# Identity transposes in TensorE's planned idle time, with a new load model and a new search of the order

## The chip, the cores and the metric

The kernel runs on one core of one Trainium2 chip. The metric is the device time of one execution in microseconds (us): the median of several runs, with one profiled execution beside them.

## What is computed

Everything is float32 at the interface. An attention over 4 batches, 8 heads, 576 positions and 64 dimensions with rotary embedding is followed by two dense blocks over the 2304 tokens:

```python
q_rot, k_rot = rotate(q), rotate(k)
scores = q_rot @ k_rot.T / sqrt(64)
attn = exp(scores - max); attn = attn / (sum(attn) + 1e-9)
x = attn @ v                                    # 2304 tokens x 512
x = ((x @ w1) * (x @ w2)) @ w3 @ w_out          # d_ff 1024
h = maximum(maximum(x @ m1, x @ m2), x @ m3)    # d_ff 768
out = h @ m_out                                 # 2304 x 512
```

## The kernel before, in words

Heads are worked on in 16 pairs (two heads side by side on 128 partitions). Every operand of a matmul is split into a high and a low part in a rounded format, and three products of parts are summed (TERMS), so one logical product is three matmuls.

For each pair there are these steps. `prepare` (line 517) loads the rotated halves of keys and queries (tiles qk; for pair 1 a tile named early), multiplies by the tables of cosines and sines (tabs, line 542), adds (544) and splits (548, 549) into the tile st. `prepare_v` splits the values (559, 561). `score` (567) makes scores into the PSUM tiles s (two of them, two banks each), VectorE takes the row maximum (590), ScalarE the exponential (593). The last 64 rows of both heads are scored together (the common score, operand z). `move` (620) transposes probabilities on TensorE against the identity (`tr`, 597; tile t), ScalarE and VectorE split them into pt (636, 637), and `values` (641) multiplies by v into pv. `collect` and `rows_done` (651, 663) sum and scale the result into xh.

Beside the pairs run the weights. `convert` (418) loads 64-bit words of a weight (raw) and makes split float32 of it on ScalarE, VectorE and POOL. `fold` (463) multiplies w3 and w_out into one matrix, eight times twelve matmuls in tiles m; `gates` (486) multiplies x by w1 and w2, in m too. After the last pair the PSUM pools are exchanged (`open_left`, 734) and the two dense blocks follow (lines 779 to 1046).

Until that exchange PSUM has eight banks: four for the two s tiles, and four shared ones (`banks = Share(4)`, line 384) from which up to two m, two t and one pv take a bank each when they are first written and give it back after their last reader.

No order is written by hand. Every instruction group is a task with an engine, a duration and a priority. `Plan.order` (193) plays all tasks through a model of the engines: on each engine the ready task with the smallest priority comes next, and this gives the static order in which the program is written for each queue (PE, ACT, DVE, POOL and SP, from which all loads and stores are issued by `load`, 375). TensorE's durations are those of full pace (0.109 us for a transpose). `Plan.issue` (281) first shakes the priorities: for each number in MOVES, `move` (84) draws from it a stretch of the order and adds random amounts to some priorities there. The list MOVES holds the numbers that a search kept. Of loads the model says:

```python
if k.tail:                                        # lines 253 to 255
    dma = max(dma, end + 0.65) + 1.2 * k.tail     # tail: 0.82 for 288 KB, 1.46 for a weight's 512 KB
    end = dma + 0.8
```

The identity (ident, line 392, load at line 706) is the second load issued.

Of the kernel before, what the change touches and what calls it, by code (L numbers as in the profile page):

```python
# [10 lines left out]
F32 = mybir.dt.float32  # L11
# [18 lines left out]
TN = 384  # L30
NU = NT // TN
NG = NU // 2

# [8 lines left out]


MOVES = (
# [24 lines left out]
)  # L71


# [9 lines left out]

def move(prio, place, seed):

    d = draws(seed)

    def uni():
        return (next(d) >> 11) * (1.0 / 9007199254740992.0)

    by = (0.1, 0.3, 0.6, 1.5)[next(d) >> 62]
    share = (0.01, 0.03, 0.1, 0.3)[next(d) >> 62]
    parts = (1, 8, 32, 128)[next(d) >> 62]
    width = len(prio) / parts
    lo = uni() * (len(prio) + width) - width
    hi = lo + width
    if parts == 1:
        share *= 0.3
    for i in range(len(prio)):
        if lo <= place[i] < hi and uni() < share:  # L100
            x = uni() + uni() + uni() + uni() - 2.0
            prio[i] = prio[i] + by * 1.7 * x


class Task:
    __slots__ = ("eng", "dur", "emit", "prio", "tail", "deps", "after", "out", "next", "fresh", "shared", "num", "lock")


class Buf:
# [26 lines left out]
class Plan:  # L136
# [6 lines left out]
    LAT = {"PE": 0.05, "ACT": 0.035, "DVE": 0.035, "POOL": 0.08, "SP": 0.1, "HOST": 0.0}  # L143
    LAP = {"PE": 0.0, "ACT": 0.1, "DVE": 0.08, "POOL": 0.04, "SP": 0.0, "HOST": 0.0}
    DRAIN = 0.165

    def __init__(self):
        self.tasks, self.rings = [], []
# [6 lines left out]
    def add(self, eng, dur, emit, r=(), w=(), part=(), deps=(), prio=0.0, tail=0.0, lock=None):  # L155


        k = Task()
        k.eng, k.dur, k.prio, k.tail = eng, dur, prio, tail
        k.lock = eng == "POOL" if lock is None else lock  # L160
        k.num, k.out, k.next = len(self.tasks), [], []
        need = set(deps)
        after, fresh = set(), []
        for b in r:
            need.update(b.writers)
        for b in list(w) + list(part):
            if b.first is None:
                b.first = k
                fresh.append(b)
        for b in w:  # L170
            need.update(b.users)
        for b in part:
            after.add(b.first)
        need.discard(k)
        after.discard(k)
        for b in list(r) + list(w) + list(part):
            b.users.append(k)
        for b in list(w) + list(part):
            b.writers.append(k)
        k.deps, k.after = need, after  # L180
        k.fresh = [b for b in fresh if b.ring.share]
        k.shared = list({id(b): b for b in list(r) + list(w) + list(part) if b.ring.share}.values())

        def go():
            for b in fresh:
                b.t = b.make(b.slot)
            emit()

        k.emit = go
        self.tasks.append(k)  # L190
        return k

    def order(self, prio):

        tasks, LAT, LAP = self.tasks, self.LAT, self.LAP
# [4 lines left out]
        for k in tasks:  # L200
            for b in k.shared:
# [2 lines left out]
                live[b.ring] = 0  # L204
                free.setdefault(b.ring.share, [(0.0, n) for n in range(b.ring.share.slots)])
                wait.setdefault(b.ring.share, [])
        clock = dict.fromkeys(LAT, 0.0)
        soon = {e: [] for e in clock}
        now = {e: [] for e in clock}
        dma, port, done = 0.0, 0.0, []  # L210
        for k in tasks:
            if not left[k.num]:
                heapq.heappush(soon[k.eng], (0.0, k.num))
        while len(done) < len(tasks):
            best = None
# [28 lines left out]
                live[b.ring] += 1  # L244
            if k.lock:
                at = max(at, port)
            end = at + k.dur
            if k.lock:
                port = end
# [1 line left out]
            if e == "PE":  # L251
                end += self.DRAIN
            if k.tail:
                dma = max(dma, end + 0.65) + 1.2 * k.tail
                end = dma + 0.8
            done.append(k)
            for b in k.shared:
# [16 lines left out]
            for o in k.next:  # L274
                ready[o.num] = max(ready[o.num], at)
                left[o.num] -= 1
                if not left[o.num]:
                    heapq.heappush(soon[o.eng], (ready[o.num], o.num))
        return clock["PE"], done, slot

    def issue(self):
        for ring in self.rings:
            if ring.share:
                for a, b in zip(ring.all, ring.all[1:]):
                    if ring.inorder:
                        b.first.after.add(a.first)
                continue
            for n in range(ring.bufs, len(ring.all)):
                b = ring.all[n]
                if b.first is not None:  # L290
                    b.first.deps.update(ring.all[n - ring.bufs].users)
        for k in self.tasks:
            k.after -= k.deps
            for d in sorted(k.deps, key=lambda d: d.num):
                d.out.append(k)
            for d in sorted(k.after, key=lambda d: d.num):
                d.next.append(k)
        prio = [k.prio for k in self.tasks]
        place = {k.num: i for i, k in enumerate(self.order(prio)[1])}
        for seed in MOVES:  # L300
            move(prio, place, seed)
        best = self.order(prio)
        for b, n in best[2].items():
            b.slot = n
        for k in best[1]:
            k.emit()

# [23 lines left out]
def fused_kernel(ctx, tc, qk, vv, cs, w3t, wo, w12, m2, wo2, out):  # L331
# [70 lines left out]
    rb_r = ring(ap, [128, S], F32, "rb")  # L402
    x_r = [ring(ap, [128, n], F32, f"x{i}_") for i, n in enumerate(PN)]
    s_r = ring(ps_a, [128, 2, 512], F32, "s", 2)
    t_r = ring(ps_m, [128, 512], F32, "t", 2, banks)
    pv_r = ring(ps_m, [128, 512], F32, "pv", 1, banks)

# [189 lines left out]
    def tr(o, x):  # L597
        pe.transpose(o, x, ident.t)  # L598

    def inverse(p):  # L600

        sm, prio = sms[p], 2 * p + 2.3
# [100 lines left out]
    for p in range(NP):  # L703
# [5 lines left out]
        for part in range(2):  # L709
# [4 lines left out]
            for j in range(2 + part):  # L714
                score(p, part, j)
            attend(p, part)
    attention = list(plan.tasks)

    for i in range(2):
# [397 lines left out]
```

## Time and profile before

| what | value |
|---|---|
| median of 3 runs | 935.26 us (934.38 to 936.12) |
| the profiled execution: time of its own | 933.76 us |
| its span, first to last instruction | 931.7 us |
| PE busy | 892.7 us, 96% |
| DVE busy | 601.5 us, 65% |
| ACT busy | 495.5 us, 53% |
| POOL busy | 397.6 us, 43% |
| mean granted TensorE clock | 0.992 |

PE is TensorE's matmuls, PEld its weight loads, DVE VectorE, ACT ScalarE, SP the queue of SyncE. Busy shares are averages over the span; the stretches of the section below take it apart. [...] The granted clock is a share of TensorE's full clock. A row's bracket says how long the engine was idle before it and what ended that.

### The profile page before, as it was taken

To read this page: it belongs to the slowest core of one execution; us is meant where nothing else is said; L and a number is where in the kernel's file an instruction comes from. 1 tells how busy PE (TensorE), PEld (TensorE's weight loads), DVE (VectorE), ACT (ScalarE), POOL (GpSimd) and SP (SyncE) were. 2 spreads that over 40 slices of the span, in tenths; PEclk is the share of its full clock that TensorE was granted. 3 is DMA by queue.
4 is the path that set the end of the run, shared out by engine and by line. 5 is a ranking of instruction groups with operands and counts; after the bars stand their busy time and mean duration, and the time that the engine had idled before them with its cause. 6 is when DMAs were issued, how large, how long until landed. Compare 5 with 4: busy or idle time off the path is not lost.

```text
span 931.7 us, 16391 instructions
## 1 busy us (share of the span) xinstructions
PE 892.7 (96%) x6018; PEld 836.9 (90%) x6018; DVE 601.5 (65%) x1048; ACT 495.5 (53%) x1108; POOL 397.6 (43%) x387
## 2 busy tenths in 40 slices
PE   2788989999999999999999999999999999999998
PEld 1577879998999999999998999999999999999886
DVE  6788888886666676567657233656788478578300
ACT  3688888886666667576655132534423333334411
POOL 2778887787745567352110000434653333232000
PEclk9799999999999999999999999999999999999999
DMA  7244556463322223311048343333333214155511
GB/s 276 85 126 164 177 187 200 128 188 101 100 91 75 69 84 99 100 41 32 27 146 273 117 142 92 103 101 96 91 91 130 63 46 147 46 184 175 214 62 68
DMA packets 61088, 110.32 MB, mean 118 GB/s; under 512 B 6736, under 2 KB 39760, under 8 KB 61008
## 3 DMA queue, kind: packets, MB, share of 16 engines
q1 hardware_dynamic: 61008, 109.28, 36.4%
q8 instruction: 47, 0.77, 0.4%
q14 instruction: 33, 0.27, 0.1%
HBM read 83.76 MB, written 25.50 MB: 117 GB/s over the span
## 4 chain that ended last, share of the span: by engine, by line
PE 86%; DVE 6%; ACT 2%; DMA 2%; issue 2%; POOL 1%; SPq 0%; DVEq 0%; ACTq 0%
PE q L373 46%; PE m L373 17%; PE t L598 9%; PE s L373 7%; PE pv L373 7%; DVE sm L590 1%; DVE pt L637 1%; ACT pt L636 1%; DVE cw L439 1%; DMA qk__118<-in_qk_dram 1%; DMA raw<-in_w_dram 1%; DVE raw L437 1%; DMA wq_d<-fl 1%; DVE early L542 0%; DMA wp<-wq_d 0%
## 5 line engine op out<-in xcount | busy, mean ns | idle before, releaser
L637 DVE TENSOR_TENSOR pt<-t,pt 128x320 fp32r<-128x320 f32 (+3 forms) x256 | 131.9, 527 | 58.4 <-ACT pt L636 54.1
L636 ACT CAST pt<-t 128x320 fp32r<-128x320 f32 (+3 forms) x256 | 112.5, 459 | 52.1 <-PE t L598 36.1
L373 PE MATMUL pv<-pt,v 128*128 128x256 f32 (+1 forms) x576 | 115.4, 317 | 4.5 <-DVE pt L637 3.6
L590 DVE TENSOR_REDUCE sm<-s 128x1 f32<-128x576 f32 x144 | 104.2, 749 | 17.3 <-PE s L373 16.4
L373 PE MATMUL q<-gt,wp 128*128 128x384 f32 x576 | 100.0, 334 | 0.0
L373 PEld LDWEIGHTS q<-gt,wp 128*128 128x128 f32 x576 | 99.8, 188 | 0.0
L373 PE MATMUL s<-st 64*128 64x288 f32 x768 | 74.2, 320 | 21.2 <-ACT st L548 13.1
L373 PEld LDWEIGHTS pv<-pt,v 128*128 128x128 f32 x576 | 83.5, 190 | 11.4 <-DVE pt L637 7.5
L373 PEld LDWEIGHTS s<-st 64*128 64x128 f32 x768 | 56.9, 193 | 35.3 <-ACT st L548 13.1
L959 ACT COPY tmp<-q 128x384 f32<-128x384 f32 x54 | 25.9, 480 | 92.6 <-PE q L373 92.1
L373 PE MATMUL q<-yc__7828,u 128*128 128x384 f32 x378 | 72.2, 340 | 0.0
L373 PE MATMUL q<-yc__8073,u 128*128 128x384 f32 x378 | 71.2, 340 | 0.0
L373 PE MATMUL q<-yc__7521,u 128*128 128x384 f32 x378 | 70.5, 340 | 0.0
L972 POOL TENSOR_TENSOR tmp<-tmp 128x384 f32<-128x384 f32 x27 | 30.2, 1119 | 86.9 <-ACT tmp L959 86.9
L373 PEld LDWEIGHTS q<-yc__8073,u 128*128 128x128 f32 x378 | 67.1, 188 | 0.1
L373 PEld LDWEIGHTS q<-yc__7828,u 128*128 128x128 f32 x378 | 67.2, 188 | 0.0
L373 PEld LDWEIGHTS q<-yc__7521,u 128*128 128x128 f32 x378 | 67.1, 188 | 0.0
L373 PE MATMUL q<-tail,tail 128*128 128x512 f32 x216 | 49.1, 389 | 0.0
L373 PEld LDWEIGHTS q<-tail,tail 128*128 128x128 f32 x216 | 40.5, 188 | 8.4
L985 DVE TENSOR_TENSOR tmp<-q,tmp 128x384 f32<-128x384 f32 x54 | 29.8, 554 | 16.3 <-PE q L373 16.2
L900 POOL TENSOR_TENSOR yx<-yc__7521 128x384 f32<-128x384 f32 x2 | 2.7, 1336 | 88.1 <-DVE yc__7521 L884 85.8
L1045 ACT COPY ga<-q 128x512 f32<-128x512 f32 x18 | 10.6, 588 | 54.8 <-PE q L373 46.7
(1282 smaller groups left out, 2149.9 us busy)
## 6 DMA issues: line engine op xcount, KB each, us to landing
gt<-g_d SPq DMA_DIRECT2D x24, 384.0 KB
raw<-in_m_dram SPq DMA_DIRECT2D x72, 128.0 KB
raw<-in_w_dram SPq DMA_DIRECT2D x16, 512.0 KB
h_d<-top SPq DMA_DIRECT2D x36, 192.0 KB
tail<-h_d SPq DMA_DIRECT2D x36, 192.0 KB
raw<-in_wo_dram SPq DMA_DIRECT2D x12, 512.0 KB
raw<-in_w3t_dram SPq DMA_DIRECT2D x12, 512.0 KB
vr<-in_vv_dram SPq DMA_DIRECT2D x16, 320.0 KB
```

Of the source, the lines that this page charges most:

```text
L373: pe.matmul(o, a, b, start=start, stop=stop, **kw)
L437: add("DVE", 0.42, lambda: dve.tensor_scalar(low_word(), low_word(), 29, None, ALU.logical_shift_right), part=[raw], deps=raw.writers, pri ...
L439: add("DVE", 0.69, lambda: dve.scalar_tensor_tensor(u(), u(), 3, low_word(), ALU.logical_shift_left, ALU.bitwise_or), r=[raw], w=[w], prio ...
L590: add("DVE", c_dve(S), lambda s=s, col=col: dve.tensor_reduce(sm.t[:, 0, col:col + 1], s.t[:, :, :288], axis=AX.XY, op=ALU.max, negate=Tru ...
L598: pe.transpose(o, x, ident.t)
L636: h = add("ACT", c_evac(n), lambda: act.copy(hi(), t.t[:rows, a:a + n]), r=[t], w=[pt], prio=prio)
L637: add("DVE", c_dve(n), lambda: dve.tensor_tensor(low(), t.t[:rows, a:a + n], f32(hi()), ALU.subtract), r=[t], part=[pt], deps=[h], prio=prio)
L900: k11 = add("POOL", c_pool(TN), lambda z=z, kk=kk: pool.tensor_tensor(z.t[:, 0], f32(yc.t[:, A11, kk, HI]), f32(yc.t[:, A11, kk, LO]), ALU ...
L959: add("ACT", c_evac(TN), lambda: act.copy(d.t, ps(o)), r=[accs[o]], w=[d], prio=prio)
L972: add("POOL", c_pool(TN), lambda: pool.tensor_tensor(s5.t, s1.t, s5.t, ALU.add), r=[s1], w=[s5], prio=prio)
L985: add("DVE", c_dve(TN), lambda: dve.tensor_tensor(e.t, ps(o), e.t, ALU.add), r=[accs[o]], w=[e], prio=prio)
L1045: add("ACT", c_evac(512), lambda acc=acc, o=o: act.copy(o.t, acc.t), r=[acc], w=[o], prio=P2 - 2)
```

## The change

Between two TensorE tasks the planner's model leaves idle time where the later task isn't ready. The change writes transposes of the identity ahead of the later task, as many as fill 0.8 of that modelled gap at 0.109 us each, counting idle time from 4.5 us on. This ends at `plan.last`, a task of no duration that waits, like pair 3's first row maximum, for pair 3's first score. The transposes write to a PSUM tile of their own, idle, which takes one of the four shared banks from the start until `plan.last`. Nothing reads it. The model itself begins at 0.7 us instead of 0, charges loads 1.9 times their tail instead of 1.2 while less than 5.0 us of load time have gone by, and 0.9 afterwards. `move` has a second kind of shake (one amount added to neighbouring tasks), and MOVES is another list, 318 numbers instead of 233, so the order of every queue differs.

```diff
+IDLE = 3
 MOVES = (
...
 def move(prio, place, seed):
...
+    if next(d) >> 63:
+        by, width = (0.3, 1.0, 3.0, 10.0)[next(d) >> 62], 1 << (next(d) >> 61)
+        lo = int(uni() * (len(prio) + width)) - width
+        x = uni() + uni() + uni() + uni() - 2.0
+        for i in range(max(lo, 0), min(lo + width, len(prio))):
+            prio[i] = prio[i] + by * 1.7 * x
+        return
...
 class Plan:
+    EARLY, FILL = 4.5, 0.8
...
         def go():
+            self.ahead(k.idle)
             for b in fresh:
                 b.t = b.make(b.slot)
             emit()
...
     def order(self, prio):
-        clock = dict.fromkeys(LAT, 0.0)
+        clock = dict.fromkeys(LAT, 0.7)
+        idle, idling = {}, True
...
+            if k is self.last:
+                idling = False
+            if e == "PE" and idling:
+                idle[k] = max(0, int(self.FILL * (at - max(clock[e], self.EARLY)) / 0.109))
             end = at + k.dur
...
             if k.tail:
-                dma = max(dma, end + 0.65) + 1.2 * k.tail
+                dma = max(dma, end + 0.65)
+                dma += (1.9 if dma < 5.0 else 0.9) * k.tail
                 end = dma + 0.8
...
     def issue(self):
         best = self.order(prio)
+        for k, n in best[3].items():
+            k.idle = n
...
     s_r = ring(ps_a, [128, 2, 512], F32, "s", 2)
+    idle_r = ring(ps_m, [128, 512], F32, "idle", 1, banks)
     t_r = ring(ps_m, [128, 512], F32, "t", 2, banks)
...
+    bank = idle_r.new()
+    def ahead(n):
+        for _ in range(n):
+            tr(bank.t[:, :128], ident.t)
+    plan.ahead = ahead
+    plan.first = add("PE", 0.0, lambda: None, w=[bank], prio=-9)
...
             attend(p, part)
+        if p == IDLE:
+            plan.last = add("PE", 0.0, lambda: None, r=[bank], deps=[k for b in sms[p].users[:1] for k in b.deps], prio=-9)
```

## Rows read from the trace of the kernel before

**Rows 1.** The page, part 2, whole span: granted clock in 40 slices (tenths).

```profile
PEclk9799999999999999999999999999999999999999
```

**Rows 2.** Busy time by stretch (us; PE, PEld, DVE, ACT, POOL, clock, DMA share, GB/s).

```profile
4.50:13.14 8.64, 0.00 (x1) 0.00 (x1) 5.71 (x9) 2.76 (x5) 0.00 (x0) 1.00 0.98 357
13.14:26.10 12.96, 7.57 (x37) 6.25 (x38) 10.34 (x12) 6.31 (x14) 6.84 (x6) 1.00 0.52 206
26.10:35.38 9.28, 7.58 (x57) 5.69 (x55) 8.75 (x14) 6.82 (x16) 7.00 (x7) 1.00 0.00 0
35.38:38.36 2.98, 0.01 (x2) 0.00 (x1) 2.95 (x5) 1.56 (x4) 1.35 (x2) 0.65 0.39 110
38.36:50.10 11.74, 9.58 (x46) 7.82 (x47) 7.68 (x15) 7.30 (x17) 9.46 (x8) 0.51 0.70 223
50.10:64.30 14.20, 11.78 (x88) 9.33 (x87) 12.84 (x22) 11.97 (x30) 11.57 (x11) 1.00 0.25 71
64.30:84.40 20.10, 17.38 (x115) 14.22 (x115) 18.70 (x31) 15.93 (x40) 16.89 (x15) 1.00 0.61 195
84.40:96.40 12.00, 11.98 (x83) 9.86 (x83) 9.43 (x18) 11.16 (x27) 11.89 (x11) 1.00 0.32 100
96.40:140.00 43.60, 40.71 (x298) 34.09 (x297) 37.24 (x64) 36.52 (x90) 36.78 (x30) 1.00 0.56 189
140.00:928.00 788.00, 786.03 (x5301) 749.65 (x5299) 487.88 (x867) 392.64 (x869) 295.07 (x298) 1.00 0.34 110
```

**Rows 3.** The same view, around the lower clock after 35 us.

```profile
35.40:37.00 1.60, 0.00 (x0) 0.00 (x0) 1.57 (x2) 0.67 (x1) 1.33 (x2) 0.77 0.62 168
...
40.00:49.00 9.00, 7.88 (x39) 6.61 (x40) 5.32 (x10) 4.74 (x14) 8.36 (x7) 0.50 0.69 230
49.00:50.00 1.00, 1.00 (x6) 0.83 (x6) 0.98 (x3) 0.92 (x2) 0.00 (x1) 0.54 0.88 302
```

**Rows 4.** Timeline of PE, the transposes from 24.7 us (start, duration).

```profile
24.70 0.41 PE L598 MATMUL t<-ident,p__182 128*128 128x128 f32 x1
...
24.90 0.42 PE L598 MATMUL t<-ident,p__208 128*128 128x128 f32 x1
...
26.45 0.27 PE L598 MATMUL t<-ident,p__182 128*128 128x128 f32 x1
...
26.55 0.27 PE L598 MATMUL t<-ident,p__208 128*128 128x128 f32 x1
```

**Rows 5.** Groups by form, PE, 38.3 to 50.1 us and 50.1 to 64.

```profile
L373 PE MATMUL s<-st 64*128 64x288 f32 x24 | 4.8, 480 | 4.4 <-ACT p__349 L593 4.2 <-ACT p__389 L593 0.2
...
L373 PE MATMUL s<-st 64*128 64x288 f32 x24 | 2.1, 309 | 0.0
```

**Rows 6.** Chain that ended last, shares by line, 13:26 and 38:50.2 us.

```profile
by line: DVE early L542 34.5%; PE s L373 26.1%; DVE sm L590 16.1%; PE t L598 6.7%; ACT p__208 L593 6.5%; DVE st L549 5.9%; DVE v L561 5.7%; ACT pt L636 4.6%; issue 1.8%
...
by line: PE s L373 27.8%; PE t L598 25.7%; PE pv L373 8.7%; ACT p__349 L593 7.7%; issue 7.0%; ACT pt L636 6.9%; DVE sm L590 6.2%; ACT p__389 L593 6.0%; ACT st L548 4.6%; ACT ws__177 L441 4.3%; ACT rt L608 1.2%; DVE sm L605 1.1%; ACTq L636 0
```

**Rows 7.** Timeline of DVE, the first row maximum.

```profile
15.53 1.42 DVE L590 TENSOR_REDUCE sm<-s 128x1 f32<-128x576 f32 x2 [0.52 <-PE s L373]
```

**Rows 8.** Busy time by stretch, tile m alone (the folds).

```profile
64.30:84.40 20.10, 6.64 (x24) 4.16 (x24) 0.00 (x0) 1.17 (x2) 1.00 0.61 195
84.40:96.40 12.00, 6.05 (x24) 4.22 (x24) 0.00 (x0) 0.58 (x1) 1.00 0.32 100
```

**Rows 9.** Chain that ended last, pieces before 140 us (start, us, what).

```profile
3.54 6.00 DMA qk__118<-in_qk_dram
...
16.95 4.49 DVE early L542 x3
...
125.39 5.86 DMA raw<-in_w_dram
```

**Rows 10.** Timeline, who waited for the first loads.

```profile
3.50 0.68 ACT L539 ACTIVATE tabs__121<-tabs__107 128x576 f32<-128x576 f32 x1 [1.49 <-DMA tabs__107<-in_cs_dram]
...
6.36 0.76 DVE L542 TENSOR_TENSOR qk__113<-qk__113,tabs__107 128x576 f32<-128x576 f32 x1 [6.36 <-DMA qk__113<-in_qk_dram]
```

More of the change, by code (lines that the diff above doesn't have):

```diff
@@ L105 @@
 class Task:
-    __slots__ = ("eng", "dur", "emit", "prio", "tail", "deps", "after", "out", "next", "fresh", "shared", "num", "lock")
+    __slots__ = ("eng", "dur", "emit", "prio", "tail", "deps", "after", "out", "next", "fresh", "shared", "num", "lock", "idle")
 class Buf:
@@ L145 @@
     DRAIN = 0.165
+    EARLY, FILL = 4.5, 0.8
+    ORDERS = 2
     def __init__(self):
@@ L160, in add @@
         k.lock = eng == "POOL" if lock is None else lock
-        k.num, k.out, k.next = len(self.tasks), [], []
+        k.num, k.out, k.next, k.idle = len(self.tasks), [], [], 0
         need = set(deps)
@@ L278, in order @@
                     heapq.heappush(soon[o.eng], (ready[o.num], o.num))
-        return clock["PE"], done, slot
+        return clock["PE"], done, slot, idle
     def issue(self):
```

54 rows, old and new, of the table MOVES are left out of this document.

## The prediction

> **What bounds the kernel now.** I read the page first, for the granted clock: it stands at 9 in all slices but one near the start [rows 1]. Then I cut the span into stretches at the places where PE starts, falls silent, or changes its pace [rows 2]. The reader is to see three regimes. From 140 us to the end of the matmuls PE is busy 786.03 of 788.00 us at the full clock: 1.97 us of idle are left in 85% of the span, so nothing that the change does there can bring much. Before 13.14 us no matmul runs at all. Between lie 127 us in which PE stands idle for 20.3 us: 5.39, 1.70, 2.97, 2.16, 2.42, 2.72 and 0.02 us up to 96.40 us, where pair 3's first score starts, and 2.89 us from there to 140. There VectorE is busy 10.34 of 12.96, 8.75 of 9.28 and 12.84 of 14.20 us: the front is a chain through VectorE and ScalarE, with PE in it now and then.
>
> [...]
>
> **The change, part by part.** Durations come from the profiled execution, 933.76 us (span 931.7), 1.50 us below the median of the runs, 935.26 us. About 0.2%, 1.9 us, is what a measurement of this kernel can tell from no change.
>
> *1. The second stretch at the lower level goes.* In 38.0 to 50.2 us the chain that ended last lies on PE for 27.8 + 25.7 + 8.7 = 62.2% [rows 6], 7.6 us of 12.2. At double pace half of that leaves the path: **-3.8 us**. Bounds: 0, if VectorE's own queue then ends last everywhere, and -4.8, half of PE's whole busy time there.
>
> *2. The first one goes.* In 13 to 26 us the chain has 26.1 + 6.7 = 32.8% on PE, 4.3 us. Of the first score's 1.6 us only the 0.52 us is worth anything for which VectorE stood idle before its first row maximum [rows 7], since after it the chain runs through VectorE's own queue for 4.49 us [rows 9]. The rest, 2.7 us (the common score and the first four transposes), halves: 1.3. Together **-1.8 us**; bounds 0 and -3.8, half of the stretch's busy time.
>
> *3. The added transposes.* The planner puts 0.8 of each modelled gap after 4.5 us into them. Taking the real gaps for the modelled ones: 8.64 us before the first score and 17.4 after it, 26.0 us, x 0.8 / 0.109 = some 190 transposes, 63 of them ahead of the first score. At the full level they start 0.10 to 0.11 us apart [rows 4] and fill the 0.8 that they should; at the lower one 0.21. With the first c us of the first block at the lower level the block takes c + (63 - c/0.213) x 0.109 = 6.9 + 0.49c us, against the 8.64 us there are: it delays nothing until c passes 3.6, and by 4.8 us where it never rises. They stand in PE's own queue, so what is late behind one is a score or a transpose, then VectorE's maximum or ScalarE's copy. One rise came within 1.75 us of the first transposes [rows 4], the other after 9 us of nearly dense work [rows 3], so both ends are open. I take **+0.4 us**, a little of the first block; bounds 0 and +4.8. After 50 us the cover is that VectorE and not PE ends last; a gap planned where there is none costs the fill's length, 0.1 us per transpose.
>
> *4. The bank.* Of four shared banks one is gone until pair 3. Two for t and one for pv remain, and before 64.3 us nothing else asks. From 64.3 to 96.4 us the folds (m) do, with 6.64 + 6.05 = 12.7 us of PE [rows 8]. A fold that can't get a bank is put later, and in its place PE idles only where nothing else is ready: VectorE is then the bound until 84 us and PE has 2.72 us idle anyway; from 84.4 to 96.4 us it has none [rows 2]. Bounds 0 and half of the folds' time, +6.3, since one bank can still serve them in turn with t. I take **+0.5**, nearer to 0, because the order is planned with three banks in view and folds fill where PE is otherwise free.
>
> *5. The order and the load model.* All queues (PE, VectorE, ScalarE, POOL, SP) are ordered anew, under a model in which early loads are slower and later ones faster. The old model has the first half of pair 0's keys landed at 0.42 (issue) + 0.65 + 1.2 x (0.82 + 0.4 + 0.82) + 0.8 = 4.3 us, after one table and ident; the trace has VectorE waiting for it until 6.36 us [rows 10], and the new constants give 0.7 + 0.42 + 0.65 + 1.9 x 2.04 + 0.8 = 6.4. So ScalarE's and VectorE's first work is put in a truer order, where now VectorE takes three multiplications for pair 1 in 4.49 us of the path [rows 9] before it serves pair 0. Gain bound: that piece, -4.5. Loss bound: a weight load that lands late like the one of 5.86 us at 125.39 us [rows 9], +5.9, as later loads are now planned a quarter shorter. I take **-1.0**: half of PE's wait, or less, around that piece; the tables land at 3.50 us and set where it can start [rows 10].
>
> Sum: -3.8 - 1.8 + 0.4 + 0.5 - 1.0 = -5.7. 933.76 - 5.7 = 928.1; with the 1.5 us between that execution and the median, **929.6 us**.
>
> [...] The rows show transposes on both sides of the rise before 26.1 us [rows 4], with matmuls of a score just ahead of them, so they don't say which of the two raised the clock. [...]
>
> **The rivals.**
> *Fill that doesn't raise the clock (slower).* Place: the blocks ahead of the first score and of the scores before 50 us. Price: +4.8 us for the first block; the later gaps at the lower level, 5.39 + 2.97 + 2.16 = 10.5 us, get 8.4 us of fill planned and 16.4 needed, 5.9 beyond the gap, of which I count half since VectorE has slack behind PE there: +3; items 1 and 2 are not earned, and items 4 and 5 give -0.5. 935.26 + 7.3 = 942.5. It decides where the lower level outlasts the first 3.6 us of a block in every gap. For it: 10 us of nearly dense work at 0.50 before 50 us [rows 3]. Against: rows 4.
> *The bank or the new order costs what the clock gives.* Folds idle for their 6.3 us, or one load wait of 5.9 on the path: 929.6 + 6 = 936. For: from 84.4 us on PE is full and m has half of it. Against: the planner sees it.
> *The change doesn't hold the clock.* Fills follow modelled gaps at 0.8, and in a real gap like 35.38 to 38.36 us the model may see none, so that one lower stretch stays. Then item 1 is missing: 929.6 + 3.8 = 933.4.
> *The order gives more.* The piece of 4.49 us leaves the path: 929.6 - 3.5 = 926, and with the full 8.6 us of clock 923.
>
> **How the numbers follow.** The forecast 0.58 (faster), the larger gain 0.08 (faster), a stretch that stays 0.14 (0.08 faster, 0.06 same), bank or order 0.10 (0.04 same, 0.06 slower), fill without effect 0.10 (slower). Faster 0.74, same 0.10, slower 0.16. The range goes from 923, the larger gain with the whole clock, to 936.5, which takes in the stretch that stays and most of the bank's case; left out are the first rival and tails, 0.18.
>
> **What would show it.** Items 1 and 2: no stretch at 0.50 between 20 and 60 us, 24 score matmuls in about 2.1 us from the first on, the first transposes of pair 0 0.11 us apart. Item 3: some 190 transposes of ident alone before about 90 us, the first 60 ahead of a first score at 12.5 to 13.5 us; wrong if that score waits for PE and not for ScalarE. Item 4: m at work between 60 and 90 us with PE idle there no more than 2.7 us. Item 5: the first score by 13 us and no VectorE piece of 4 us ahead of pair 0's second maximum. Pair 3's first score should come about 5.5 us earlier, near 91 us, and from there to the end the distance stay 835 us; were pair 3 early and the end not, the prediction would be wrong.

## The result, and the profile after

The changed kernel takes 940.34 us (median of 5 runs, 938.29 to 942.83) against 934.38 us of the kernel before (5 runs, 932.72 to 936.12): the ratio is 1.0061 with the 95% interval 1.0035 to 1.0087. It is slower by 0.6%, where a gain of 0.6% was forecast. The profiled execution of after took 940.34 us, with a span of 938.6.

The page of after, parts 1 and 2: the engines' busy time, then the granted clock in 40 slices.

```profile
PE 918.8 (98%) x6303; PEld 862.9 (92%) x6303; DVE 601.4 (64%) x1048; ACT 494.8 (53%) x1108; POOL 398.3 (42%) x387
...
PEclk9999999999999999999999999999999999999999
```

The low slice of [rows 1] is gone, and PE carries 285 matmuls more. All of them are fills, as the group by form of PE from 0 to 100 us and PE's timeline at the start show:

```profile
L625 PE MATMUL idle<-ident 128*128 128x128 f32 x285 | 38.5, 287 | 3.8 <-DMA ident<-in_cs_dram 3.8
...
3.84 11.71 PE L625 MATMUL idle<-ident 128*128 128x128 f32 x81 [3.84 <-DMA ident<-in_cs_dram]
15.48 1.24 PE L399 MATMUL s<-st 64*128 64x288 f32 x12
```

81 fills run before anything else, and the first score starts at 15.48 us (before: 13.14). Busy time by stretch of after, the columns as in [rows 2]:

```profile
4.50:8.00 3.50, 3.50 (x19) 3.50 (x18) 0.76 (x1) 0.69 (x1) 0.00 (x0) 1.00 0.92 284
8.00:9.00 1.00, 1.00 (x6) 1.00 (x5) 0.76 (x2) 0.69 (x1) 0.00 (x0) 1.00 0.96 309
9.00:10.00 1.00, 1.00 (x10) 1.00 (x9) 1.00 (x3) 0.00 (x0) 0.00 (x0) 1.00 1.00 378
...
38.40:50.10 11.70, 10.40 (x91) 9.20 (x88) 9.96 (x16) 7.92 (x20) 9.08 (x9) 1.00 0.65 198
...
140.00:480.00 340.00, 338.72 (x2784) 319.49 (x2785) 240.08 (x453) 238.12 (x599) 185.89 (x167) 1.00 0.30 97
...
490.00:500.00 10.00, 7.53 (x56) 7.05 (x54) 7.47 (x16) 5.72 (x10) 0.00 (x0) 1.00 0.72 229
500.00:505.00 5.00, 4.94 (x20) 4.16 (x21) 2.08 (x5) 1.29 (x3) 0.00 (x0) 0.66 0.48 166
...
520.00:530.00 10.00, 8.21 (x41) 6.57 (x40) 3.78 (x7) 0.99 (x2) 0.00 (x0) 1.00 0.36 107
530.00:540.00 10.00, 8.52 (x60) 7.99 (x59) 2.71 (x5) 1.73 (x4) 0.00 (x0) 1.00 0.79 244
```

Three things are to be seen. The clock column has no 0.50 left. In the first block, for which the column prints 1.00 throughout, 6 fills lie in a microsecond up to 9 us and 10 in the next one: the pace rises to the full level in a run of nothing but transposes. And a new hole has opened far behind the place of the change: from 490 to 540 us PE now idles for 2.47 + 0.06 + 1.79 + 1.48 = 5.8 us and works at a clock of 0.66 from 500 to 505. The kernel before has hardly a gap there, 0.44 us in all. Its own rows for the same time:

```profile
490.00:500.00 10.00, 10.00 (x55) 8.69 (x54) 8.18 (x17) 5.43 (x10) 0.00 (x0) 1.00 0.86 291
500.00:520.00 20.00, 19.56 (x106) 17.10 (x105) 11.84 (x21) 6.77 (x11) 0.00 (x0) 1.00 0.73 230
520.00:540.00 20.00, 20.00 (x146) 19.71 (x145) 4.17 (x8) 3.22 (x7) 0.00 (x0) 1.00 0.23 79
```

This is just behind the exchange of the PSUM pools, where weights are folded (tiles q, rawc, fl, wq_d) and the last gates (ga, g_d) are made. The chain that ended last, after, from 476 to 545 us (start, us, what):

```profile
482.80 5.64 DMA rawc<-in_wo_dram
...
490.12 3.50 DMA rawc<-in_w3t_dram
...
495.03 4.58 DMA g_d<-ga
...
500.06 15.38 PE q L399 x72
...
516.55 3.88 DMA wq_d<-fl
...
522.80 5.78 DMA wq_d<-fl
```

and the same view of before, one piece of it:

```profile
480.36 20.41 PE q L373 x126
```

Before, PE's own matmuls, gates and folds, carry the chain from 480 to 501 us while the weights land beside them. In after the chain runs for most of this time through transfers, one after another, and PE waits for what depends on them. PE's waits of after from 92 to 940 us (us in total, times, longest):

```profile
PE q L399 <- ACT ga L527: 3.9, 2, 2.5
PE q L399 <- DVE fl L815: 1.8, 2, 1.3
```

At pair 3 the changed kernel looks early: its first score starts at 92.6 us, 3.8 us ahead of before. But less work has been done by then. Tile m alone, after, the columns of [rows 8]:

```profile
64.30:84.40 20.10, 3.28 (x12) 2.10 (x12) 0.00 (x0) 0.58 (x1) 1.00 0.44 140
84.40:96.40 12.00, 4.54 (x18) 3.24 (x18) 0.00 (x0) 0.58 (x1) 1.00 0.54 187
```

Counted up to pair 3's first score, 24 fold matmuls are done after and 48 before. Twelve of them take 2.73 us where they run in a row (the chain of after has "PE m L399 x12" of 2.73 us at 89.94), so the 24 that are missing are a debt of 5.5 us, which comes due where PE is nearly always busy. Early by 3.8 and in debt by 5.5, the changed kernel is 1.7 us behind at pair 3, by this estimate.

### The profile page after: what moved, and what is told of

The parts are those of the page before. It is cut to its first block, busy times and chain, and to the rows that moved or that the text cites. A ratio compares the mean times of both kernels' runs of the same rounds, so it can differ in the third digit from the quotient of the medians.

```text
span 938.6 us, 16938 instructions
## 1 busy us (share of the span) xinstructions
PE 918.8 (98%) x6303; PEld 862.9 (92%) x6303; DVE 601.4 (64%) x1048; ACT 494.8 (53%) x1108; POOL 398.3 (42%) x387
## 4 chain that ended last, share of the span: by engine, by line
PE 83%; DMA 7%; DVE 5%; ACT 2%; issue 1%; SPq 1%; POOL 0%; DVEq 0%; ACTq 0%
PE q L399 44%; PE m L399 17%; PE t L625 8%; PE pv L399 7%; PE s L399 7%; DVE pt L674 1%; DMA vr<-in_vv_dram 1%; DMA wq_d<-fl 1%; DVE cw L466 1%; DMA raw<-in_w_dram 1%; DVE sm L617 1%; PE idle L625 1%; SPq L402 1%; DVE raw L464 1%; DMA raw<-in_w3t_dram 1%
## 5 line engine op out<-in xcount | busy, mean ns | idle before, releaser
L399 PE MATMUL pv<-pt,v 128*128 128x256 f32 (+1 forms) x576 | 112.0, 313 | 1.7 <-DVE pt L674 0.9
L399 PE MATMUL q<-gt,wp 128*128 128x384 f32 x576 | 100.0, 334 | 0.0
L399 PEld LDWEIGHTS q<-gt,wp 128*128 128x128 f32 x576 | 99.8, 188 | 0.0
L399 PEld LDWEIGHTS pv<-pt,v 128*128 128x128 f32 x576 | 82.1, 189 | 6.5 <-DVE pt L674 2.3
L399 PE MATMUL q<-yc__8099,u 128*128 128x384 f32 x378 | 71.1, 338 | 0.0
L399 PE MATMUL q<-yc__8377,u 128*128 128x384 f32 x378 | 70.5, 338 | 0.0
L399 PE MATMUL q<-yc__7815,u 128*128 128x384 f32 x378 | 70.1, 338 | 0.0
L399 PE MATMUL s<-st 64*128 64x288 f32 x768 | 68.8, 309 | 0.0
L399 PEld LDWEIGHTS q<-yc__8377,u 128*128 128x128 f32 x378 | 66.5, 188 | 0.3
L399 PEld LDWEIGHTS q<-yc__8099,u 128*128 128x128 f32 x378 | 66.6, 188 | 0.0
L399 PEld LDWEIGHTS q<-yc__7815,u 128*128 128x128 f32 x378 | 66.5, 188 | 0.0
L399 PEld LDWEIGHTS s<-st 64*128 64x128 f32 x768 | 53.4, 184 | 11.6 <-issue 6.5
L399 PE MATMUL q<-tail,tail 128*128 128x512 f32 x216 | 49.1, 389 | 0.0
L399 PEld LDWEIGHTS q<-tail,tail 128*128 128x128 f32 x216 | 40.6, 188 | 8.4
L477 DVE TENSOR_TENSOR gt<-gt 128x768 fp32r<-128x768 f32 x24 | 26.3, 1096 | 27.9 <-ACT gt L476 25.7
L939 POOL TENSOR_TENSOR yx<-yc__7815 128x384 f32<-128x384 f32 x2 | 2.7, 1338 | 95.9 <-DVE yc__7815 L923 94.0
L625 PE MATMUL idle<-ident 128*128 128x128 f32 x285 | 38.5, 287 | 3.8 <-DMA ident<-in_cs_dram 3.8
```

The source lines that it names most:

```text
L399: pe.matmul(o, a, b, start=start, stop=stop, **kw)
L477: add(eng, c_dve(n) if eng == "DVE" else c_pool(n), lambda: e.tensor_tensor(sel()[:, LO], f32(sel()[:, LO]), f32(sel()[:, HI]), ALU.subtract),
L939: k11 = add("POOL", c_pool(TN), lambda z=z, kk=kk: pool.tensor_tensor(z.t[:, 0], f32(yc.t[:, A11, kk, HI]), f32(yc.t[:, A11, kk, LO]), ALU ...
```

## The experiments

Most of these kernels have a fixed order. The planner is taken out and the order, the bank numbers and the fill counts stand in the program as lists, so that parts of two orders can be put together exactly. "Front" is all that is issued up to the exchange of the PSUM pools, "rest" what is issued behind it. The edit they share stands here once; below, the contents of such lists are told in words in the diff.

```diff
     def issue(self):
...
-        best = self.order(prio)
...
-        for k in best[1]:
-            k.emit()
+        for k, n in IDLES:
+            self.tasks[k].idle = n
+        for k in ORDER.split():
+            self.tasks[int(k)].emit()
```

All ratios are against the kernel before, run beside them on the same chip, with 95% intervals.

**The fill alone.** The order of before throughout, with fills in its own gaps until the first fold; the bank is given back there. 219 fills, 70 of them ahead of the first score.

```diff
-ORDER: as the changed planner makes it, bank held until pair 3
+ORDER: that of before, bank held until the first fold
+IDLES = ((27, 70), (32, 22), (37, 4), (40, 1), (51, 6), (59, 1), (62, 3), (65, 16), (73, 11), (80, 12), (104, 2), (110, 3), (118, 3), (122, 5), (157, 38), (162, 10), (170, 1), (175, 7), (189, 3), (198, 1))
```

> The kernel before, instruction for instruction in its order, with the added transposes alone: 219 of them by the rule of the change (0.8 of the gap that the new model sees in this order), in a bank that is free until the first fold and given back there. If the front is in part bound by TensorE's pace, as predicted: 3.8 + 1.8 us gained less some 1.5 for a first block that is too long while the clock is low, 930 to 932 us. Rival (the front is bound by VectorE, ScalarE and loads whatever the clock): 933 to 936 us.

Measured: 932.72 us, ratio 0.9988 (0.9968 to 1.0008). The clock stays up; busy time by stretch of this kernel:

```profile
35.40:38.40 3.00, 3.00 (x31) 2.83 (x31) 2.51 (x5) 2.91 (x7) 1.72 (x1) 1.00 0.51 141
38.40:50.10 11.70, 11.70 (x99) 10.29 (x97) 10.20 (x18) 7.93 (x20) 11.55 (x11) 1.00 0.74 227
```

Pair 3 starts at 92.8 us in its profile with all 48 folds done, 3.6 us early and with no debt. At the end only 1.1 us (0.12%) of it are seen, which this interval doesn't tell from nothing. Three kernels below have the same front and reach pair 3 at 94.4, 94.7 and 95.2 us, so this profile is the lowest of four; some 2 us is the fair figure for that mark.

**A shorter first block.** Is the gain lost because the block of fills holds up the first score (14.1 us against 13.1)?

```diff
-IDLES = ((27, 70), (32, 22),
+IDLES = ((27, 55), (32, 22),
```

> f1_fill_alone with 55 instead of 70 transposes ahead of the first score. In f1 that block ended after the first score's operands were there (first score at 14.1 us, 13.1 in the kernel before). My theory: the first score comes at about 13 us and the time falls by 1 us, to 931 to 932 us. Rival: ScalarE and VectorE set the pace from there whatever the first score does: no change from f1, 932.5 to 933.5.

Measured: 932.5 us, 0.9988 (0.9975 to 1.0002). The first score comes at 12.9 us, and nothing follows from it: pair 0's common score comes at 22.9 us and pair 3 at 94.1. The length of the first block isn't what holds the front.

**Fewer fills everywhere.** 134 fills: 52 in the first block, 20 in the longest later one, 0.6 of the others.

```diff
-IDLES = ((27, 70), (32, 22), (37, 4), (40, 1), (51, 6),
+IDLES = ((27, 52), (32, 13), (37, 2), (40, 1), (51, 3),
```

> f1_fill_alone with 134 instead of 219 transposes (52 ahead of the first score, 20 instead of 38 in the longest later gap, 0.6 of the others). Theory: the clock stays at the full level and pair 3 starts at 92 to 94 us as in f1, so 931 to 933 us, at best 1 us under f1. Rival: with open gaps the clock falls again: 934 to 936 us, with a granted clock under 1 between 35 and 50 us.

Measured: 931.78 us, 0.9978 (0.9962 to 0.9994), faster than before. Pair 3 starts at 92.0 us. The clock of the stretch from 13 to 26 us falls to 0.87 in this profile, without harm.

**Only the late fills.** 46 fills, all from the gap ahead of 38 us on; none before.

```diff
-IDLES = ((27, 52), (32, 13), (37, 2), (40, 1), (51, 3), (59, 1), (62, 1), (65, 9), (73, 6), (80, 7),
+IDLES = ((80, 7),
```

> The order of before and 46 fills alone, all from the gap ahead of 38 us on: 20 there, the rest in eleven later gaps; none ahead of the first score or in the first stretch at the lower clock. Theory 'only the second stretch is bound by TensorE': first score where before has it, at 13.1 us, the clock at 1.00 from 38 to 50 us, pair 3 at 92 to 93 us and a time of 930 to 932. Rival 'the early fills carry the clock over': without them the stretch from 38 us stays at 0.50, pair 3 at 96 us, 933 to 934.

Measured: 931.89 us, 0.9975 (0.9962 to 0.9989): no less than with 134 or 219 fills, and with a sixth of the changed kernel's. The scores by form from 13 to 23.5 us, here and in the fill alone, then busy time by stretch in its longest fill and behind it:

```profile
L406 PE MATMUL s<-st 64*128 64x288 f32 x24 | 4.6, 488 | 15.2 <-ACT st L582 13.2 <-ACT p__183 L627 1.7 <-DVE st L583 0.2
...
L406 PE MATMUL s<-st 64*128 64x288 f32 x24 | 2.1, 309 | 0.0
```

```profile
34.60:35.40 0.80, 0.80 (x5) 0.80 (x5) 0.80 (x1) 0.67 (x1) 0.80 (x1) 0.50 0.44 61
35.40:36.00 0.60, 0.60 (x5) 0.60 (x4) 0.57 (x2) 0.00 (x0) 0.46 (x2) 0.50 0.80 273
36.00:37.00 1.00, 1.00 (x7) 1.00 (x6) 1.00 (x2) 0.39 (x1) 0.00 (x0) 0.50 0.31 115
37.00:38.40 1.40, 1.40 (x11) 1.23 (x9) 1.40 (x4) 1.40 (x4) 0.27 (x1) 0.77 0.33 32
...
38.40:50.10 11.70, 10.11 (x79) 8.18 (x79) 9.84 (x17) 8.53 (x23) 11.56 (x10) 1.00 0.75 245
```

The first stretch is left at the lower pace: 24 score matmuls take 4.6 us, against 2.1 in the fill alone, and the time is no worse for it. Nor does pair 1 come later: its first score starts at 38.38 us here and at 38.36 before, against 36.0 to 40.3 us in the six profiles of kernels that have before's front with early fills. So no worth of the first stretch is to be seen (this kernel and the one with 134 fills differ by 0.03%, good to about 0.2%), and the second, with the gaps behind it, is worth all that is. Of the 46 fills 20 stand in the second stretch's own gap; what the other 26 do alone was not tried. From pair 1's first score at 38.4 us to its common score it takes 10.2 us (38.4 to 48.6) instead of 13.1 (38.4 to 51.5). The second block shows the clock itself: it had fallen before the fills, and it comes back while PE does 20 transposes and nothing else.

**The changed order without its fills.**

```diff
 def ahead(n):
-        for _ in range(n):
-            tr(bank.t[:, :128], ident.t)
+        pass
```

> The changed kernel with its order, its bank and its load model, and no added transposes at all. My theory: the fills hold the clock at the full level and cost little by themselves, so without them TensorE falls to the lower level again in the first 50 us and the time is the same or higher, 941 to 945 us. Rival (the fills stand in front of ready work and are the loss): faster by 2 us or more, 935 to 938 us, with the first score well before 15 us.

Measured: 947.51 us, 1.0144 (1.0114 to 1.0175). In the changed order the fills are worth 0.83%, 7.8 us; its order, with the bank set aside in it, is 13 us slower than that of before. Busy time by stretch of this kernel, with the clock in the third column from the end:

```profile
38.40:50.10 11.70, 8.85 (x58) 6.96 (x57) 10.05 (x17) 8.14 (x21) 8.40 (x8) 0.85 0.70 220
64.30:84.40 20.10, 17.20 (x103) 14.23 (x103) 16.45 (x25) 13.11 (x33) 16.15 (x14) 0.84 0.47 140
84.40:96.40 12.00, 10.52 (x69) 8.62 (x68) 9.91 (x18) 10.61 (x25) 7.59 (x6) 0.86 0.29 80
```

With 24 of the 48 fold matmuls put off PE has gaps up to 96 us, 2.9 and 1.5 us in the last two rows, and the clock reads 0.84 and 0.86 there. In the order of before, with all 48 there, it reads 1.00 [rows 2, rows 8]. So a part of what the fills repair may be what the new order broke; no run puts those folds back alone.

**Fewer fills in the changed order.** 161 fills, the rest as changed.

```diff
-            self.ahead(k.idle)
+            self.ahead(int(0.6 * k.idle))
```

> The changed kernel with 0.6 of its added transposes in every gap (48 instead of 81 ahead of the first score) and nothing else touched. If the number of fills is oversized and they delay work: 2 us or more below the changed kernel's ratio of 1.0061, 936 to 938 us. If they cost nothing as they are: the same as the changed kernel, or up to 3 us above it where the clock falls in a gap left open.

Measured: 944.11 us, 1.0106 (1.0071 to 1.0141), slower than with all of them by 0.45%, good to about 0.4. Here fewer fills cost time, where in the order of before they cost none.

**Which half is slow.** After's front with before's rest, before's front with after's rest, and the front of the fill alone with after's rest.

```diff
-ORDER: after's throughout
+ORDER: after's up to the exchange, before's behind it
```

> All tasks up to the exchange of the PSUM pools in the order of the changed kernel, fills included; all later tasks in the order of the kernel before. My theory: some 5 us of the 6 us lost lie behind the exchange (480 to 540 us, where TensorE waits for loads), so this takes 934 to 936 us. Rival (the loss is in the front or in the fills): 939 to 941 us, as the changed kernel.

Measured: 936.63 us, 1.0025 (1.0006 to 1.0043).

```diff
-ORDER: after's throughout
+ORDER: before's up to the exchange, after's behind it; no fills
```

> The mirror image: the order of the kernel before up to the exchange of the PSUM pools, without fills and bank; the order of the changed kernel behind it. My theory: it keeps the loss behind the exchange, 938 to 940 us. Rival (front): 933 to 935 us, as the kernel before.

Measured: 943.42 us, 1.0088 (1.0053 to 1.0123).

```diff
-ORDER: before's throughout (the fill alone)
+ORDER: before's up to the exchange, after's behind it; the same fills
```

> f1_fill_alone up to the exchange of the PSUM pools, the changed kernel's order behind it. My theory: the loss behind the exchange doesn't hang on the front, so 4 to 8 us above f1: 937 to 941 us. Rival (h2 was bad because its front ran at the lower clock): 933 to 935.

Measured: 942.0 us, 1.0083 (1.0058 to 1.0107). So after's rest costs 0.36% on its own front (1.0061 against 1.0025, 3.4 us) and 0.95% (8.9 us) behind the front of before with fills. After's front costs 0.37% (3.5 us) against the front of before with fills, 1.0025 against 0.9988. Each half of the new order is slower beside a half of the old one. The two costs don't add up, though: after's two halves together, 1.0061, are no slower than after's rest behind the filled front of before, 1.0083. Busy time by stretch of the last kernel:

```profile
480.00:500.00 20.00, 16.53 (x120) 15.71 (x119) 11.72 (x22) 9.26 (x16) 0.00 (x0) 1.00 0.76 237
500.00:520.00 20.00, 19.16 (x89) 15.92 (x88) 9.47 (x16) 5.90 (x11) 0.00 (x0) 0.92 0.53 161
520.00:540.00 20.00, 17.96 (x101) 15.97 (x101) 6.59 (x11) 3.35 (x7) 0.00 (x0) 0.93 0.63 199
```

**Why the rest is slow.** The tasks get as priorities their places in after's order, the planner runs once with one number changed, and the rest of its order goes behind the front of the fill alone. In the second kernel the same is done with the places in before's order and the new load model.

```diff
-                dma += (1.9 if dma < 5.0 else 0.9) * k.tail
+                dma += (1.9 if dma < 5.0 else 1.2) * k.tail
```

> As c3_fill_after_rest, but the order behind the exchange comes from the changed kernel's own order taken as priorities and planned again with later loads at 1.2 instead of 0.9 of their tail. If the shorter loads of the model made that order bad: 934 to 938 us, 4 or more below c3. Rival (it is this particular order, whatever the load model): 940 us or more.

Measured: 932.76 us, 0.9989 (0.9974 to 1.0005). The 8.9 us are gone, and PE's idle time from 480 to 540 us falls from 6.4 to 2.4 us. Its busy time by stretch:

```profile
480.00:500.00 20.00, 18.81 (x135) 17.97 (x134) 13.24 (x25) 10.16 (x18) 0.00 (x0) 1.00 0.81 260
500.00:520.00 20.00, 18.76 (x97) 15.91 (x96) 11.02 (x20) 6.26 (x12) 0.00 (x0) 1.00 0.52 153
520.00:540.00 20.00, 20.00 (x135) 19.27 (x134) 7.53 (x14) 4.97 (x10) 0.00 (x0) 1.00 0.74 218
```

```diff
-                dma = max(dma, end + 0.65) + 1.2 * k.tail
+                dma = max(dma, end + 0.65)
+                dma += (1.9 if dma < 5.0 else 0.9) * k.tail
```

> f1_fill_alone up to the exchange of the PSUM pools, then the order of the kernel before taken as priorities and planned again with the changed load model (0.9 for later loads). If the load model alone makes the order behind the exchange bad: 936 to 941 us. Rival (the model's factor does little, the search's choice does it): 932 to 934 us.

Measured: 934.93 us, 0.9997 (0.9978 to 1.0017), between the two times that were expected and 0.9 us above the fill alone by the ratios, not to be told from it. So the short loads by themselves spoil little of before's order; it is the order that was chosen under them that costs time, and planning it once more with 1.2 takes the cost away. Planning it once more is not the cure by itself: after's planner, given the places of its own order and 0.9, returns the same order but for 8 of 1489 places on PE and 3 of 963 on ScalarE. Which of its placings does the harm is not shown. Whether a load that lands late is enough for it is not shown either: under 0.9 a 512 KB load of tail 1.46 is planned to land 0.65 + 0.9 x 1.46 + 0.8 = 2.8 us behind its issue (3.2 us under 1.2), and w_out's took 5.64 us on the chain of after; but one of 512 KB took 5.86 us on the chain of before, too, at 125.39 us [rows 9].

**Why the front is slow.** First the bank alone: before's places, the old load model, the bank held until pair 3 with 251 fills, planned once, and before's rest behind it.

```diff
+    idle_r = ring(ps_m, [128, 512], F32, "idle", 1, banks)
...
+        if p == IDLE:
+            plan.last = add("PE", 0.0, lambda: None, r=[bank], deps=[k for b in sms[p].users[:1] for k in b.deps], prio=-9)
```

> The mirror image: the front of the kernel before, planned again with its own order as priorities, its old load model, fills and the bank set aside until pair 3; old rest. If the bank is the cause: slower than f1_fill_alone by 3 us or more, 936 us or above. If not: 932 to 934, as f1.

Measured: 943.61 us, 1.0108 (1.0086 to 1.013). Pair 3 starts at 97.7 us, with all 48 fold matmuls done; from 92 us on the transposes' waits for pt, the split probabilities, come to 8.6 us in seven waits (0.9 us in two in the fill alone). 11 us over the fill alone is the price of the bank in an order that wasn't made for it.

Then after's places without the bank: four banks, the new load model, fills until the first fold, before's rest.

```diff
-            plan.last = add("PE", 0.0, lambda: None, r=[bank], deps=[k for b in sms[p].users[:1] for k in b.deps], prio=-9)
+ORDER: planned with four banks, bank held until the first fold
```

> As h1_after_front (changed front, old rest), but the front is planned with the changed kernel's own order as priorities and with all four banks for t, pv and m; the fills use a bank that is free until the first fold and stop there. The planner then puts 18 instead of 8 fold tasks ahead of pair 3's first score. If the bank is what the front lost: 932 to 934 us, 3 below h1. Rival (the newly searched order of the front is slower by itself): 936 to 938, as h1 or worse.

Measured: 934.65 us, 1.0017 (1.0002 to 1.0033), between the two times that were expected. With four banks 54 fold matmuls are done at pair 3 (95.0 us); after's front, with before's rest behind it too, has 24 (93.2 us). With after's places the bank holds the folds back, then; with before's places, in the kernel above, it held back none but made pair 3 late. At the end the two fronts differ by only 0.08%, 0.8 us, which the intervals don't tell from nothing. The front with four banks loses elsewhere: PE idles for 4.0 us between 92 and 140 us, at a clock of 0.96.

```profile
92.00:140.00 48.00, 44.04 (x299) 36.38 (x299) 38.65 (x66) 37.82 (x92) 36.16 (x31) 0.96 0.53 170
```

What is left, 0.29% (2.7 us) over the fill alone, this front costs without the bank.

Last, the bank and after's places with 1.2 for later loads, with before's rest and with its own.

```diff
-                dma += (1.9 if dma < 5.0 else 0.9) * k.tail
+                dma += (1.9 if dma < 5.0 else 1.2) * k.tail
```

> A front planned from the ranks of the new order with the bank and the fills, but with 1.2 instead of 0.9 for later loads; behind the exchange of the PSUM pools the order of before. It is the kernel of the run with after's front and before's rest, except for the load factor under which the front was planned. Theory 'the search under short loads made the front worse too': 932 to 933.5, the 3.5 us between that run and the fill alone come back. Rival 'the bank holds the folds up, whatever the loads': 936 to 937 as with after's front, with 24 m matmuls ahead of pair 3.

Measured: 942.21 us, 1.0085 (1.0067 to 1.0103). Neither time that was expected came, and nothing here says that the short loads made the front slow: with 1.2 it is slower by another 5.6 us. 24 fold matmuls are done at pair 3 (95.9 us), and busy time by stretch shows 3.8 us of gaps where before has 0.9:

```profile
140.00:300.00 160.00, 156.18 (x1271) 145.80 (x1270) 117.22 (x215) 115.05 (x284) 105.38 (x91) 1.00 0.39 124
```

> The whole change, planned from the ranks of its order with one number changed: later loads at 1.2 instead of 0.9. Theory 'the load factor with its search makes the part behind the exchange slow': that part costs nothing any more, so this kernel stands within 1 us of the one that has the same front and the order of before behind it. Rival 'the bank shifts the folds and so the exchange itself': some 3 us above it, and PE idle for over 3 us between 480 and 540 us.

Measured: 943.46 us, 1.0096 (1.0081 to 1.0111), 1.0 us over the one before it by the ratios. So a rest planned with 1.2 does little harm behind this front too, as it does none behind the other.

What these kernels can't do is to part the bank from the list of shakes. An order that the planner makes anew from old places, under another model, was never chosen among others, and that alone can cost time: the last front did no more than change a number and lost 5.6 us. Each such run bounds the cost of its edit from above. What of the front's 3.5 us is the bank's, between nothing and all of it, stays open.

## Why the prediction was wrong

The forecast added -5.6 us of clock, +0.4 of fills, +0.5 of bank and -1.0 of order. The clock gave less, 1 to 2 us, and the order, with the bank in it, took some 7 us where it was to give 1: item 5 is the step that decided. The 8.6 us of clock behind the range's 923 are half of PE's 7.57 + 9.58 us in the two stretches [rows 2]; no run shows them, and the fastest of these kernels is 0.25%, 2.3 us, under before.

By the ratios the 0.61% come apart in one order of steps as follows, each good to between 0.2 and 0.3%: the fill on the old order -0.12%, the new order and load model in the front +0.29, the bank +0.08, the rest +0.36. Taken in another order the steps have other sizes: behind the filled front of before the rest alone costs 0.95.

*Item 1, the second stretch (-3.8): right where it was placed.* From pair 1's first score to its common score 2.9 us go in the kernel with late fills (13.1 to 10.2). In the one with after's rest behind the filled front it is 3.7 (13.1 to 9.4). At the end of the kernel 2.3 us are left (0.25%, interval 0.11 to 0.38). The chain's share of PE by double pace was a fair measure there: 24 score matmuls take 4.8 us at the clock of 0.50 and 2.1 in the stretch after [rows 5].

*Item 2, the first stretch (-1.8): wrong, none of it is seen,* and 0 was the lower bound that was named. That PE ran at the lower pace here, where the clock column prints 1.00, is read from its transposes, 0.20 us apart at 24.70 us and 0.10 at 26.45 [rows 4]. The late fills leave it so and lose nothing. PE has a third of the chain there [rows 6], but halving a piece of a chain takes time away only until the next path ends last, and VectorE is busy 10.34 of 12.96 us there [rows 2]. This reason is argued; no run makes VectorE's work there less.

*Item 3, the added transposes (+0.4): about right in size, not in number.* 285 instead of 190: by the same rule the order of before gets 219 up to its first fold, and the new order has more to fill up to pair 3. The first block took 81 and reached the full clock after about 5 us, later than the 3.6 us up to which it was to cost nothing. The mark that the first score must not wait for PE is missed by a little: ScalarE's operand is done at 14.95 us, the block ends and the score starts at 15.48, and without fills it starts at 14.81. Its cost in the order of before is the 1.2 us between the fill alone and the late fills, which the intervals don't separate.

*Item 4, the bank (+0.5): its size stays open, and the step that failed is "one bank can still serve them in turn".* In the order that was chosen with the bank half of the folds, 24 of 48, move behind pair 3, 5.5 us of PE's work; the bound of 6.3 was there, and the value was taken near to 0. In the order of before one bank does serve all of them, but pair 3 and the end come late, the end by 11 us against the fill alone. The mark for pair 3, "near 91 us", looked only at the time and not at the work done, and might have passed 92.6 for a gain. The other half of that sentence, that the distance to the end must stay 835 us, caught it: 938.6 - 92.6 is 846.0 against 931.7 - 96.4 = 835.3.

*Item 5, the order and the load model (-1.0): the wrong sign, and the step that decided.* In the front a truer model of the first loads gave no earlier score. ScalarE takes the values ahead of pair 0's second operand, as before; but their load is now issued behind pair 1's, at 5.78 us instead of 4.02, and ScalarE waits for it. ScalarE's timeline of before, then of after:

```profile
10.37 0.72 ACT L559 CAST v<-vr 128x640 fp32r<-128x640 f32 x1
12.41 0.67 ACT L548 CAST st<-qk__118 128x576 fp32r<-128x576 f32 x1 [1.32 <-DVE qk__118 L544]
...
13.65 0.73 ACT L586 CAST v<-vr 128x640 fp32r<-128x640 f32 x1 [2.59 <-DMA vr<-in_vv_dram]
14.28 0.67 ACT L575 CAST st<-qk__119 128x576 fp32r<-128x576 f32 x1
```

Behind the exchange the new order costs 3.4 us on its own front. There PE waits at the end of a chain of transfers that w_out's load of 5.64 us opens; a late weight load was named as the bound of a loss (5.9) and set aside. That this load alone makes the loss is not shown, only that the order chosen under the short loads does. The sentence "nothing that the change does there can bring much" was true of gains and was read as if it were true of losses: where PE is full for 786 us, an order that is worse shows.

*The rivals.* "The bank or the new order costs what the clock gives" is the one that came: it was priced at 936 and given a tenth. Its two halves, folds and one late load, were seen, as alternatives. The trace of after shows both; the runs price the order, and leave the bank's own part open. "Fill that doesn't raise the clock" falls, though the time of 942.5 that it gives is close: the clock rises in a block of nothing but transposes, near 9 us in after and near 37 us in the kernel with late fills. A right time would have been no proof of a rival's mechanism.

## What to carry to other kernels

Fill an idle TensorE only where it ends last: with 62% of the chain on PE at the lower clock the fill paid, with 33% none of it was seen, and 46 transposes from the second stretch on did what 219 did. That kernel, 931.89 us against 934.26 of the kernel before, is faster than both that this document compares. Where a change comes with a new order, price the order by its worst stretch and not by the place it was made for, and compare two kernels at a mark by the work done up to it, not by its time alone. A load model that a planner trusts is a claim about every queue. Here the short loads did little to an order that was already chosen, but the order that was searched under them left PE waiting where it had been full.

## What was not expected of the hardware

In runs of nothing but float32 transposes the clock came up: in the kernel with late fills it stands at 0.50 from 34.6 to 37.0 us while PE does transposes only, and reads 1.00 from 38.4 on; in after, where the first 81 fills have no other matmul ahead of them, their pace goes from 6 to 10 in a microsecond near 9 us. One front, with the same instructions in the same order, reaches pair 3 between 92.8 and 95.2 us in four profiles: they are 2.4 us apart, so a single profile of the front settles nothing under that. Behind a hole the clock was low, too: after 2.47 us of idle PE from 490 to 500 us the rows of after show 0.66 from 500 to 505, where those of before, with no idle time from 490 to 500, show 1.00 from 500 to 520.
